# Odd heads' copies of k of three segments by DMA instead of by the vector engines, no unread products beside turns, and a new set of due times in an interleaved attention and feed-forward kernel

## The chip, the cores and the metric

The kernel runs on one core of a Trainium2 chip. The metric is device time in microseconds of one execution. Five engines work side by side, each through its own instruction stream in order: TensorE (PE, with its weight loads PEld), VectorE (DVE), ScalarE (ACT), GpSimd (POOL) and SyncE (SP), which here does nothing but issue DMAs.

## The reference, cut to what matters

Two blocks, A (attention with a memory, 32 heads of 16) and B (gated feed-forward), are applied twice in turn to x of 2048 x 512; inputs and outputs are bf16.

```
x = x + A(layernorm(x)); x = x + B(layernorm(x))     # and both once more

A: q, k, v = x @ wq, x @ wk, x @ wv                  # 32 heads, 16 columns each, 4 segments of 512 rows
   for s in 0..3:                                    # segments in order
       p = softmax(qs @ ks.T / 4 + causal mask)      # inside the segment
       a_dot = p @ vs
       a_mem = phi(qs) @ M / (phi(qs) @ z + 1e-6)    # what the earlier segments left
       o = g * a_mem + (1 - g) * a_dot               # g = sigmoid(beta), one per head
       M += phi(ks).T @ vs;  z += sum of phi(ks)
   return o @ wo
B: (gelu(x @ w_gate) * (x @ w_up)) @ w_down          # inner width 1792
```

## The kernel before, in words

One Python function, `order` (L286), writes out every engine's instruction stream itself. While it does so it keeps a clock for each engine (`Clocks`, L155) with fixed costs for each kind of instruction, and decides from these clocks what each engine gets next. The stream is fixed when the program is built; on the chip the engines follow it and wait for each other only through semaphores.

There are eight units of work, k = 0 to 7: four segments in the first application of A and B, four in the second (`Att` and `Ffn`). A segment has 512 rows in four tiles of 128. For each k:

- `Norm` makes statistics (`bn_stats`, `bn_aggr`), a scale on GpSimd, and normalized rows xn. These are turned into xnT either by a DMA transpose on SP's queue (`turn_later`) or, for the feed-forward of k = 0, 1 and 7, by TensorE (`turn_item`, L575). `turn_item` puts `FILL` = 2 products of the constant tile `warm` with nobody reading them ahead of each turn.
- q, k and v are projected (items of kind "qk" and "v") and evicted from PSUM by VectorE or ScalarE. Heads are kept in blocks of 128 rows, b = 0 to 3: each group of 32 rows holds an even head in rows 0 to 15 and an odd head in rows 16 to 31.
- `masked_copies` (L411) makes the tile kx from kf (the evicted k) by two multiplications with a mask of rows: one with the even heads' rows kept into columns 0 to C of each 3C (C = 64), one with the odd heads' rows kept into columns C to 3C. VectorE, GpSimd or ScalarE does both, whichever is free first. On VectorE and GpSimd the first copy writes 128 columns, of which the second overwrites the last 64. kx has two buffers (`kxs`) used by k in turn; for k = 0 it lies in the still empty tile of w_down. Event ("kB", k, b) says that it is there.
- `score_round` (L926) multiplies q with kf (even heads) or kx (odd heads, and both heads together) in 36 rounds of 256 columns, two rounds at a time: 18 pairs for each k. ScalarE takes the exponential (L1399), GpSimd masks the diagonal (L1346, L1351).
- `flush_item` (L943) multiplies the result with v (and with vz, a copy of halves of v that DMAs make) and hands it to VectorE for a transpose, a division and a transpose back. For k whose segment is not the first of four, the memory's part is added.
- The output projection ("wo"), the feed-forward's gate, up and down products follow. Gelu has its own phases on ScalarE.

What is ready is chosen by its due time, in units of k: `POLICY` (L69) holds some forty numbers, and `CHANGES` could give other numbers for each 20 us of the clocks, but is empty. A "qk" item is due at k - qk_due, a gate at k + gate_due + gate_step * ft, and so on; score rounds come before all others when their inputs, PSUM banks and buffers are free. Where no item is ready, the order puts in one unread product of `warm` (128 columns).

SP's queue carries, in this order of issue by its clock: loads of x and the weights, DMA transposes (xn, the exponentials of k, the memory's part), the copies for vz, and the stores. Pieces of w_o, w_gate and w_up are posted from 32 us, those of w_down after segment 0's scores.

```
PAIRED = [(ki, P * ki, C, C * ki) for ki in range(TPS)]
BY_PE = {("xnTf", 0), ("xnTf", 1), ("xnTf", NK - 1)}
FILL = 2
```

Of the kernel before, what the change touches and what calls it, by code (L numbers as in the profile page):

```python
# [18 lines left out]
P = 128  # L19
D = 512  # L20
# [11 lines left out]
VALUES = TPS * VW + 16  # L32
SCALE = DH ** -0.5
# [11 lines left out]
PAIRED = [(ki, P * ki, C, C * ki) for ki in range(TPS)]  # L45


def round_of(t):

    b, i = divmod(t, ROUNDS)  # L50
    if i == SHARED:
        return b, (0, 1), PAIRED, None
    par = int(i > SHARED)
    return b, (par,), FULL[i - par * (SHARED + 1)], DIAG[i - par * (SHARED + 1)]


BY_PE = {("xnTf", 0), ("xnTf", 1), ("xnTf", NK - 1)}
BANKS = 8
# [3 lines left out]
URGENT, SOON, NORMAL = -4.0, -1.5, 0.0  # L62
XN_BUFS = 4
BUFS = 6
FILL = 2
# [4 lines left out]
    flush_wait=60.178, piece_slack=2.474, kb_slack=40.846, mem_slack=-55.59, margin=2.052, qk_due=-2.997, e_q=-1.628,  # L70
    e_k=2.444, exp_slack=-52.211, e_slack=213.844, phi_slack=26.757, gelu_slack=17.711, act_evict=-7.207,
    first_evict=15.014, gate_step=70.271, up_due=-0.803, up_step=0.121, down_due=2.855, down_step=15.464,
    upd_due=-0.036, kb_act=30.625, vz_slack=-37.946, x_dve=-2.928, v0_due=-11.201, x1_at=-44.439, x2_at=17.127,
    x3_at=25.097, x3_load=11.502, direct=4, gelu_tiles=7, look=4.219, lag=0.576, wv_at=-5.253, xn_pool=39.635,
# [3 lines left out]
CHANGES = {  # L78
}
# [12 lines left out]
class Engine:  # L92
# [24 lines left out]
    def serve(self, now):  # L117
# [9 lines left out]
        job = min((j for j in jobs if j[0] + self.LATENCY <= start + 0.03), key=lambda j: j[0] + j[1] + (  # L127
# [123 lines left out]
class Item:  # L251


    def __init__(self, due, ready, ops, done, kind, ps, after="start"):
        self.after = after
        self.due = due if callable(due) else lambda: due
        self.ready, self.ops, self.done, self.kind, self.ps = ready, ops, done, kind, ps
        self.posted = 0.0
# [27 lines left out]
def order(pol, nc, cst, seg, wrk, psp, A_x, A_wq, A_wk, A_wv, A_wo, A_beta, B_x, B_w_gate, B_w_up, B_w_down, out):  # L286
# [88 lines left out]

    tmp_e2 = cst.tile([P, H], F32, name="tmp_e2")
# [26 lines left out]

    def on_dve_or_pool(ready, slack, later, fast, slow, emit, told):
# [6 lines left out]
    def masked_copies(ready, slack, kx, kf, told):  # L411
# [4 lines left out]
        def vector(which, eng):  # L416
            return lambda: eng.tensor_scalar(out=kx[:, :, C * which:C * which + P], in0=kf, scalar1=masks[:, which:which + 1],  # L417
                                             scalar2=None, op0=ALU.mult)
# [6 lines left out]
        ck.dve.post(ready, slack, (Port(0.35), vector(0, nc.vector), None),  # L425
                    (Port(0.35), vector(1, nc.vector), told), taken=taken)
        ck.pool.post(ready, slack + pol.kb_pool, (Port(1.57, True), vector(0, nc.gpsimd), None),
# [3 lines left out]
    def turn_later(t, slack, out, in_, landed, margin=0.0):  # L431
# [5 lines left out]
        ck.sp.post(t, slack, (1.3, lambda: nc.sync.dma_start_transpose(out=out(), in_=in_()), told))  # L437
# [40 lines left out]
    def soon(name, n=KT, part=1.0):  # L478

        t = ck.pe - 0.1 - ck.back  # L480
# [20 lines left out]
    class Norm:  # L501
        def __init__(self, key, tt0, tag, slack, free):
            self.key, self.tt0, self.tag, self.slack, self.free = key, tt0, tag, slack, free
            self.mv, self.n, self.left = None, 0, TPS
# [3 lines left out]

        def stats(self, j, ready):
            def emit():  # L510
                if self.mv is None:
                    self.mv = self.small("mv", 2)
# [3 lines left out]
            def told(t):  # L516
                self.n += 1
                if self.n == TPS:
                    self.scales(t)

            ck.dve.post(ready, self.slack, (0.66, emit, None),
# [1006 lines left out]
```

## Time and profile before

| | us |
|---|---|
| median of 3 runs (lowest to highest) | 542.2 (541.96 to 543.59) |
| the profiled execution, its own time | 543.32 |
| its span, first to last instruction | 541.6 |
| ScalarE's 288 exponentials (L1399), busy | 278.9 |
| VectorE's 18, GpSimd's 16 and ScalarE's 22 copies into kx, busy | 9.9, 27.0, 12.2 |
| SP's DMAs: 48 transposes of xn, median from issue to landing | 2.9 |

Times in the profile are counted from the span's start. A row of the timeline gives its start, its length, the engine and line, output and inputs, and in brackets how long the engine was idle before and what ended the idle time. A row of a window gives the stretch, its length, each engine's busy time in it with the number of instructions, the granted clock of TensorE (1.00 is full speed), the mean busy share of the DMA engines and GB/s. Matmuls are pipelined, and their busy time is modelled, so a busy TensorE is not one at its peak.

### The profile page before, as it was taken

What the parts mean: (1) busy time and instruction counts of PE and PEld (TensorE: products, weight loads), DVE (VectorE), ACT (ScalarE), POOL (GpSimd) and SP (SyncE); (2) the same over time, 40 slices, a digit from 0 to 9 for tenths busy, and PEclk for the clock granted to TensorE, in tenths of its full rate; (3) what the DMA queues carried; (4) which work ended last, traced back from release to release, by engine and by line L of the source; (5) the groups of instructions that cost most, each with busy time, mean ns of one, the idle gap of its engine ahead of it and who ended that gap; (6) DMA issues with size and microseconds to landing.
All of it is one profiled execution on the core that took longest, in us unless ns stands there. A gap on an engine that the chain in (4) does not pass through costs nothing.

```text
span 541.6 us, 22747 instructions
## 1 busy us (share of the span) xinstructions
PE 522.7 (97%) x10016; PEld 274.0 (51%) x10075; DVE 439.1 (81%) x814; ACT 434.3 (80%) x533; POOL 297.4 (55%) x346
## 2 busy tenths in 40 slices
PE   8899999999999999999999999999999999999997
PEld 4454555454554445554555545554465456555444
DVE  7899998899988998679987699879778786786342
ACT  5999899997998987999899899997887978910320
POOL 4887589487857986155871595716863164300000
PEclk9999999999999999999999999999999999999999
DMA  8477410620240124101332211411313014000001
GB/s 270 63 123 178 136 41 7 153 52 14 33 79 14 24 41 89 33 2 32 42 70 32 34 34 20 72 22 33 61 33 40 15 13 81 4 3 27 14 0 40
DMA packets 69141, 28.08 MB, mean 52 GB/s; under 512 B 53426, under 2 KB 69042, under 8 KB 69042
## 3 DMA queue, kind: packets, MB, share of 16 engines
q1 hardware_dynamic: 68752, 26.36, 24.5%
q8 instruction: 79, 1.29, 1.0%
q10 hardware_dynamic: 290, 0.26, 0.1%
q14 instruction: 20, 0.16, 0.1%
HBM read 9.70 MB, written 2.10 MB: 22 GB/s over the span
## 4 chain that ended last, share of the span: by engine, by line
PE 88%; DVE 6%; issue 2%; ACT 1%; DMA 1%; POOL 0%; ACTq 0%; DVEq 0%; POOLq 0%
PE ps L476 39%; PE ps L471 34%; PE ps L939 8%; PE ps L955 7%; ACT pt L1399 1%; DVE xn L544 1%; DMA xnT<-xn 1%; DVE st L514 1%; DVE x_sb L1028 1%; DMA x_sb<-in_A_x_dram 1%; PE ps L866 1%; DVE kx L417 0%; DVE st L1184 0%; DVE pt L1356 0%; DVE byq L972 0%
## 5 line engine op out<-in xcount | busy, mean ns | idle before, releaser
L1399 ACT ACTIVATE pt<-ps 128x1024 bf16<-128x1024 f32 x288 | 278.9, 1030 | 38.4 <-PE ps L939 34.1
L1346 POOL TENSOR_SCALAR_AFFINE_SELECT pt<-pt 128x256 bf16<-128x256 bf16 (+1 forms) x192 | 109.6, 584 | 132.5 <-ACT pt L1399 129.0
L1093 DVE TENSOR_TENSOR gel_sb<-gel_sb,ps 128x512 bf16<-128x512 bf16 x112 | 75.3, 683 | 33.8 <-PE ps L476 20.5
L1028 DVE TENSOR_TENSOR x_sb<-x_sb,ps 128x512 bf16<-128x512 bf16 (+1 forms) x68 | 43.1, 643 | 26.9 <-PE ps L476 16.4
L764 POOL TENSOR_SCALAR e<-e 128x512 bf16<-128x512 bf16 x39 | 61.4, 1577 | 4.6 <-ACT e L741 3.6
L476 PE MATMUL ps<-wd_sb,gel_sb 128*128 128x512 bf16 (+1 forms) x287 | 58.7, 351 | 1.5 <-issue 1.3
L972 DVE STREAM_TRANSPOSE byq<-ps 128x512 f32<-128x512 f32 x64 | 45.1, 706 | 16.1 <-PE ps L955 15.6
L471 PE MATMUL ps<-xnT,wg_sb 128*32 128x512 bf16 x916 | 56.1, 380 | 0.1
L476 PE MATMUL ps<-xnT,wu_sb 128*128 128x512 bf16 x213 | 51.1, 379 | 1.5 <-issue 1.1
L476 PE MATMUL ps<-xnT,wg_sb 128*128 128x512 bf16 x207 | 49.9, 379 | 1.6 <-issue 1.4
L471 PE MATMUL ps<-xnT,wu_sb 128*32 128x512 bf16 x888 | 51.0, 379 | 0.0
L471 PE MATMUL ps<-wd_sb,gel_sb 128*32 128x512 bf16 (+1 forms) x816 | 45.3, 361 | 0.0
L476 PEld LDWEIGHTS <-gel_sb 128*128 128x128 bf16 x300 | 27.9, 98 | 25.3 <-issue 0.4
L514 DVE BATCH_NORM_STATS2 st<-x_sb 128x6 f32<-128x512 bf16 x60 | 40.4, 673 | 0.2
L1351 POOL TENSOR_SCALAR_AFFINE_SELECT pt<-pt 64x1024 bf16<-64x1024 bf16 x26 | 32.4, 1247 | 9.8 <-ACT pt L1399 9.0
L955 PE MATMUL ps<-pt,vaug 128*32 128x256 bf16 (+2 forms) x1344 | 35.2, 238 | 1.5 <-issue 1.0
L471 PEld LDWEIGHTS <-wu_sb 128*32 128x32 bf16 x888 | 23.0, 97 | 22.3 <-issue 0.9
L955 PEld LDWEIGHTS <-vaug 128*32 128x32 bf16 x1344 | 27.6, 97 | 12.6 <-issue 4.1
L476 PEld LDWEIGHTS <-wu_sb 128*128 128x128 bf16 x226 | 20.8, 98 | 24.8 <-issue 1.2
L471 PEld LDWEIGHTS <-wg_sb 128*32 128x32 bf16 x916 | 23.4, 97 | 19.1 <-issue 1.3
L1152 ACT ACTIVATE gel_sb<-gel_sb 128x3584 bf16<-128x3584 bf16 (+1 forms) x14 | 32.4, 2351 | 0.0
L939 PE MATMUL ps<-q,kx 32*128 32x64 bf16 (+2 forms) x1120 | 31.2, 217 | 0.7 <-ACT pt L1399 0.5
(145 smaller groups left out, 892.7 us busy)
## 6 DMA issues: line engine op xcount, KB each, us to landing
vz<-vaug SPq DMA_DIRECT2D x14, 136.0 KB, 3.0
wg_sb<-in_B_w_gate_dram SPq DMA_DIRECT2D x8, 224.0 KB, 3.6
wu_sb<-in_B_w_up_dram SPq DMA_DIRECT2D x8, 224.0 KB, 2.9
wd_sb<-in_B_w_down_dram SPq DMA_DIRECT2D x7, 256.0 KB, 4.4
x_sb<-in_A_x_dram SPq DMA_DIRECT2D x3, 512.0 KB, 6.5
out_dram<-x_sb SPq DMA_DIRECT2D x12, 128.0 KB, 1.7
xnT<-xn SPq DMA_TRANSPOSE x48, 2.9
wk_sb<-in_A_wk_dram SPq DMA_DIRECT2D x2, 256.0 KB, 4.7
```

The costliest lines, as they stand in the source:

```text
L471: nc.tensor.matmul(out[r], lhsT=lhsT[:, r], rhs=rhs, start=start, stop=stop, tile_position=(0, 32 * c))
L476: nc.tensor.matmul(out, lhsT=lhsT, rhs=rhs, start=start, stop=stop)
L514: nc.vector.bn_stats(out=self.st6[:, 0, :], in_=x_sb[:, self.tt0 + j, :])
L764: lambda eng: eng.tensor_scalar(out=e[0][:], in0=e[0][:], scalar1=1.0, scalar2=None, op0=ALU.min), summed)
L939: nc.tensor.matmul(ps_all[:, bank, o + c0:o + c0 + n], lhsT=lhsT, rhs=self.q[rows, b, q0:q0 + n], start=True, stop=True, tile_position=(32 ...
L955: nc.tensor.matmul(ps()[32 * j:32 * j + 32, q0:q0 + n], lhsT=va[:, ki * VW + g:ki * VW + g + 32], rhs=pt_all[:, places[i], j, c0:c0 + n], ...
L972: nc.vector.transpose(out=self.byq[:, par, :, :].rearrange("p a c -> p (a c)"), in_=ps()[:])
L1028: ck.dve.post(ck.made(), slack, (0.15 + 0.00104 * (c1 - c0), lambda: nc.vector.tensor_tensor(out=xt, in0=xt, in1=ps()[:, 0:c1 - c0], op=AL ...
L1093: ck.dve.post(ck.made(), NORMAL, (0.683, lambda: nc.vector.tensor_tensor(out=g, in0=g, in1=ps()[:], op=ALU.mult), lambda t: (ps.read(t), e ...
L1152: return (0.205 + 0.427 * (f1 - f0), lambda: nc.scalar.activation(out=g, in_=g, func=ACT.Gelu_apprx_tanh), lambda t: self.gelu_done(t, f0, ...
L1346: nc.gpsimd.affine_select(out=view, in_=view, pattern=[[0, 4], [0, n], [1, C]], compare_op=ALU.is_ge, fill=0.0, base=C, channel_multiplier=-1)
L1399: nc.scalar.activation(out=pt_all[:, s0:s0 + 2, 2 * p:2 * p + 2, :].rearrange("p r h c -> p h r c"), in_=ps_all[:, pair[0]:pair[1] + 1, :] ...
```

## The change

1. For k = 1, 2 and 3 (`SENT`) the odd heads' rows of kx are no longer made by a masked multiplication. Four DMAs on SP's queue, one for each group of 16 rows, copy them from kf for all four blocks once all four are evicted. The rows of the even heads in these columns must be zero: VectorE zeroes them, for k = 1 and 3 (buffer 1) among the constants at the start, for k = 2 (buffer 0) in an instruction posted for 14 us. Later k in these buffers write the whole tile again by both masked copies.
2. The even heads' copy is 64 columns wide for each tile on every engine. For `SENT` it is the only one.
3. A round with odd heads waits for event ("kC", k, b) also, which the last of the four DMAs sets.
4. `FILL` is 0.
5. `POLICY` has other numbers, and `CHANGES` now has three further sets, from 80, 160 and 260 us.
6. Segment 0's gates from tile `HELD` = 5 on no longer wait for its memory update (tiles 0 to 4 of gel_sb hold segment 0's v until then), and its gates and ups are due in the order 5 to 13, 0 to 4. All gates wait until the first weights are there by the clock (`("loaded", "first")`), the down products for the last ones. An output projection waits for the half of aT that it reads.
7. Some costs of the clocks differ by a few hundredths (DMA issues 0.57 to 0.59 and 1.3 to 1.34).

Further code (tables of rounds by halves of a segment, statistics by ScalarE, a priority `CHAIN`) hangs on the tuple `HALVED`, which is empty, so that `table` gives the rounds and flushes of before.

```diff
-FILL = 2
+FILL = 0
+HELD = -(-VALUES // L)
+HALVED = ()
+SENT = (1, 2, 3)
...
-    flush_wait=60.178, piece_slack=2.474, kb_slack=40.846, mem_slack=-55.59, margin=2.052, qk_due=-2.997, e_q=-1.628,
+    flush_wait=1.624, piece_slack=0.155, kb_slack=53.547, mem_slack=-59.422, margin=2.0, qk_due=-7.042, e_q=-1.688,
...
-    kb_pool=0.131, cut_pool=-3.745, at_pool=5.073, pe_turns=0, gate_due=2.262, shun=0.829, col_gap=3.113, hold=3,
-    early=122.612, starve=0.322, near=-0.26, cap=2, soon=21.81, columns=0)
+    kb_pool=-10.364, cut_pool=0.647, at_pool=-5.829, pe_turns=0, gate_due=-18.64, shun=0.038, col_gap=0.385, hold=3,
+    early=105.4, starve=0.313, near=-1.083, cap=1, soon=20.189, columns=0, kd_slack=-0.023, zero_slack=2.11)
+STAGES = [
+    (4, 8, dict(
+        flush_wait=-28.356, piece_slack=0.165, kb_slack=13.812, mem_slack=-84.736, qk_due=-16.936, e_q=-16.571,
...
+        look=-0.727, lag=0.499, xn_pool=18.224, kb_pool=41.434, cut_pool=-4.43, at_pool=-1.122, gate_due=-0.69,
...
+    (8, 13, dict(
+        flush_wait=4.011, kb_slack=53.832, mem_slack=-53.484, qk_due=-18.021, e_q=-2.29, e_k=8.851, e_slack=302.471,
...
+        xn_pool=37.273, kb_pool=-1.463, cut_pool=-1.793, at_pool=-0.568, gate_due=-22.888, shun=-0.495, hold=0,
...
+    (13, 60, dict(
...
+        gate_due=2.674, shun=-0.495, hold=0, early=122.74, starve=0.322, near=-6.87, cap=0, soon=19.366,
+        kd_slack=2.0)),
+]
+CHANGES = {w: change for w0, w1, change in STAGES for w in range(w0, w1)}
...
+    nc.vector.memset(means[:, 0:1], -float(D) ** -1.5)
+    nc.vector.memset(means[:, 1:2], 1.0 / D)
+    nc.vector.memset(kxs[1][:, :, :, C:3 * C], 0.0)
...
+    ev["zero", 1] = ev["zero", 3] = 0.0
+    ck.dve.post(14.0, pol.zero_slack, (Port(0.95), lambda: nc.vector.memset(kxs[0][:, :, :, C:3 * C], 0.0),
+                                       lambda t: ev.update({("zero", 2): t})))
...
-    def masked_copies(ready, slack, kx, kf, told):
+    def masked_copies(ready, slack, kx, kf, even, told):
...
-            return lambda: eng.tensor_scalar(out=kx[:, :, C * which:C * which + P], in0=kf, scalar1=masks[:, which:which + 1],
-                                             scalar2=None, op0=ALU.mult)
+            n = P if which else C
+            return lambda: eng.tensor_scalar(out=kx[:, :, C * which:C * which + n], in0=kf[:, :, 0:n],
+                                             scalar1=masks[:, which:which + 1], scalar2=None, op0=ALU.mult)
...
+        if even:
+            ck.dve.post(ready, slack, (Port(0.28), vector(0, nc.vector), told), taken=taken)
+            ck.pool.post(ready, slack + pol.kb_pool, (Port(0.93, True), vector(0, nc.gpsimd), told), taken=taken)
+            ck.act.post(ready, slack + pol.kb_act, (0.51, scalar(0), told), taken=taken)
+            return
...
+            def sent():
+                parts = [32 * j + 16 for j in range(4)]
+                kf = self.kf[:].rearrange("p b (t c) -> p (b t) c", c=P)
+                kx = self.kx.rearrange("p b t c -> p (b t) c")
...
+                for r in list(parts):
+                    ck.sp.post(ck.pe, pol.kd_slack, (0.64, lambda r=r: nc.sync.dma_start(
+                        out=kx[r:r + 16, :, C:3 * C], in_=kf[r:r + 16, :, :]), told))
...
+                    if k in SENT:
+                        self.n_k += 1
+                        if self.n_k == KT:
+                            ck.at(t, lambda: ck.when(lambda: (k <= 2 or ("scores", k - 2) in ev) and ("zero", k) in ev, sent))
...
-                return Item(k + 0.61 + 0.001 * j, lambda: soon(("aT", k)),
-                            dense(ps, pairs), done, kind="wo", ps=ps, after=("aT", k, 3))
+                return Item(k + 0.61 + 0.001 * j, lambda: soon(("aTh", k, j // 2), eager=k in HALVED),
+                            dense(ps, pairs), done, kind="wo", ps=ps, after=("aTh", k, j // 2, 3))
...
-                return Item(lambda: -0.8 if phase[0] == k else k + pol.gate_due + pol.gate_step * ft,
-                            lambda: ck.has(("xnTf", k)) and (("down", k - 1) if k else ("upd", 0)) in ev,
+                return Item(lambda: -0.8 if phase[0] == k else k + pol.gate_due + pol.gate_step * place(ft),
+                            lambda: ck.has(("xnTf", k), ("loaded", "first")) and (k == 0 and ft >= HELD or (("down", k - 1) if k else ("upd", 0)) in ev),
```

More of the change, by code (lines that the diff above doesn't have):

```diff
@@ new lines, in second, with start @@
+                nc.gpsimd.tensor_tensor(out=self.rs[:, j0:j0 + n, :], in0=self.ve[:], in1=mhalf[:, 0:n, :], op=ALU.pow)
+            ck.pool.post(ready, min(self.urge(j0), URGENT), (0.25, first, None),
+                         (1.05, second, lambda t: ck.when(self.free, lambda: self.start(max(t, ck.pe), j0, n))))
+        def start(self, ready, j0, n):
+            if self.xnT is None:
+                self.xnT = seg.tile([P, KT, L], BF16, tag=self.tag, bufs=1, name="xnT")
+            for j in range(j0, j0 + n):
@@ L945, in flush_item @@
             ps = Psum()
-            number = 8 * k + 2 * b + par
+            places = self.places
+            half = L // 2
+            c0, c1 = (0, L) if h is None else (half * h, half * h + half)
+            na = (c1 - c0) // 32
+            work = []
+            for par in pars:
+                for t in used:
+                    for b2, par2, ki, q0, nq, o in TABLES[k][0][t][0]:
+                        if b2 == b and par in par2 and c0 <= q0 < c1:
+                            work.append((par, t, vz if len(par2) > 1 else self.vaug, ki, q0 - c0 + (par * half if h is not None else 0),
+                                         nq, o))
```

314 lines of the change are left out of this document (208 added, 106 removed).

## The prediction

> **What bounds the kernel now.** I read the page first: busy time and share of each engine, then the chain of waits.
>
> ```profile
> PE 522.7 (97%) x10016; PEld 274.0 (51%) x10075; DVE 439.1 (81%) x814; ACT 434.3 (80%) x533; POOL 297.4 (55%) x346
> ...
> PE 88%; DVE 6%; issue 2%; ACT 1%; DMA 1%; POOL 0%; ACTq 0%; DVEq 0%; POOLq 0%
> ```
>
> TensorE is 97% busy and 88% of the chain is its own work. An edit that frees VectorE, ScalarE or GpSimd is therefore worth only what TensorE lost by waiting for them. Where that was shows in the windows: busy us (with counts) of PE, PEld, DVE, ACT, POOL, then the clock, the DMA share and GB/s.
>
> ```profile
> 20.00:40.00 20.00, 18.28 (x427) 10.04 (x432) 18.61 (x44) 19.47 (x28) 16.84 (x19) 1.00 0.72 117
> 40.00:60.00 20.00, 19.57 (x360) 9.43 (x355) 19.27 (x35) 19.05 (x27) 13.10 (x15) 1.00 0.67 173
> 60.00:80.00 20.00, 18.61 (x462) 10.89 (x467) 19.06 (x40) 18.40 (x25) 15.42 (x18) 1.00 0.29 72
> 120.00:140.00 20.00, 18.35 (x481) 10.53 (x477) 19.57 (x40) 16.87 (x22) 16.18 (x21) 1.00 0.08 17
> 20.00:140.00 120.00, 114.01 (x2467) 61.66 (x2483) 111.84 (x215) 112.65 (x143) 91.23 (x99) 1.00 0.40 86
> 160.00:460.00 300.00, 293.56 (x6063) 152.92 (x6091) 250.58 (x455) 264.23 (x315) 173.47 (x201) 1.00 0.23 39
> ```
>
> Busy is not useful: with nothing ready the order emits products of the constant tile warm, which nobody reads. The windows of that tile alone (PE, PEld, DVE):
>
> ```profile
> 60.00:80.00 20.00, 2.59 (x54) 1.72 (x54) 0.00 (x0) 1.00 0.29 72
> 120.00:140.00 20.00, 1.88 (x29) 1.22 (x29) 0.00 (x0) 1.00 0.08 17
> 20.00:140.00 120.00, 6.93 (x126) 4.41 (x126) 0.00 (x0) 1.00 0.40 86
> 160.00:460.00 300.00, 0.00 (x0) 0.00 (x0) 0.00 (x0) 1.00 0.23 39
> ```
>
> I call idle plus unread products starvation. From 20 to 140 us it is 120 - 114.01 + 6.93 = 12.9 us; from 160 to 460 it is 300 - 293.56 = 6.4 us, or 0.43 per 20 us. At that plain rate 20 to 140 would cost 2.6, so **10.3 us** is all that a better supply can win. The two stretches that I price hold 20 - 18.61 + 2.59 - 0.43 = 3.55 us (60 to 80) and 20 - 18.35 + 1.88 - 0.43 = 3.1 us (120 to 140). The timeline says what they wait for:
>
> ```profile
> 64.73 1.46 PE L476 MATMUL ps<-wo_sb,aT 128*128 128x512 bf16 x6
> 66.12 0.40 PE L939 MATMUL ps<-q,kx 32*128 32x64 bf16 x20
> ...
> 71.79 0.51 PE L471 MATMUL ps<-warm 128*32 128x128 bf16 x24
> ...
> 78.80 1.55 PE L471 MATMUL ps<-xnT,wg_sb 128*32 128x512 bf16 x24
> ...
> 133.84 0.34 PE L471 MATMUL ps<-warm 128*32 128x128 bf16 x12
> ...
> 138.55 1.05 PE L471 MATMUL ps<-xnT,wg_sb 128*32 128x512 bf16 x16
> ```
>
> Unread products run from 71.8 until the first gate product of segment 0 at 78.8, and again from 133.8 to 138.5 before that of segment 1. The chain in front is: the segment's score rounds and their exponentials, P V, output projection (64.7), statistics, scale, normalized rows, turns, gate. It takes 14.1 us from the output projection to the gate alone.
>
> **The change part by part.** *Copies of k.* For segments 1 to 3, the windows of tile kx (PE, PEld, DVE, ACT, POOL) around their two places, then the whole window of the second place, ScalarE's two forms by themselves (busy us, mean ns), and VectorE's one (shortest, median, longest ns):
>
> ```profile
> 30.00:55.00 25.00, 0.00 (x0) 0.00 (x0) 4.39 (x8) 3.38 (x6) 3.24 (x2) 1.00 0.73 156
> 114.00:120.00 6.00, 0.00 (x0) 0.00 (x0) 1.31 (x2) 2.25 (x4) 3.13 (x2) 1.00 0.37 68
> ```
>
> ```profile
> 114.00:120.00 6.00, 5.95 (x146) 3.15 (x136) 5.39 (x11) 6.00 (x9) 5.90 (x7) 1.00 0.37 68
> ```
>
> ```profile
> L422 ACT ACTIVATE kx<-kf,masks 128x512 bf16<-128x512 bf16 x11 | 7.9, 719 | 0.0
> ...
> L422 ACT ACTIVATE kx<-kf,masks 128x256 bf16<-128x256 bf16 x11 | 5.6, 511 | 0.7 <-DVE kf L461 0.7
> ```
>
> ```profile
> L417 DVE TENSOR_SCALAR kx<-kf,masks x18: 332/566/820, 35.2 to 392.6; 128x512 bf16<-128x512 bf16 x18
> ```
>
> Twelve blocks lose the wide copy and keep one of 256 columns. On ScalarE, three blocks near 30 to 55 us: 3.38 - 3 x 0.511 = 1.85 us saved; two at 114 to 120: 2.25 - 2 x 0.511 = 1.23. VectorE shows no copy of 256 columns: it lies between half of 0.332 and 0.332; I take ScalarE's ratio, 0.511/0.719 x 0.332 = 0.24, since both shrink the same pattern. VectorE then saves 4.39 - 4 x 0.24 = 3.4 us in the first place. ScalarE is 97% and 95% busy around the first place (19.47 and 19.05 of 20), 100% at the second (6.00 of 6), and both lie ahead of a starved one, so I let ScalarE's 1.85 + 1.23 = **3.1 us** come off the two chains; each is less than the starvation behind it. Ends: 0, if VectorE's share of the chain is what sets it, and 4.6, with VectorE's 3.4 in the first place. The narrower first copies of the other segments save at most some 0.1 us each on VectorE; they lie where starvation is at the plain rate: nothing.
>
> *The zeroing.* Two memsets of 16 x 128 bf16 per partition. Nearest row: vz.
>
> ```profile
> 1.23 0.97 DVE L342 MEMSET vz<- 128x1096 uint32 x1 [0.18 <-issue]
> ...
> 2.48 0.15 DVE L374 TENSOR_REDUCE masks<-bd 128x1 f32<-128x4 f32 x1
> 3.72 0.69 DVE L1184 BATCH_NORM_STATS2 st<-x_sb 128x6 f32<-128x512 bf16 x1 [1.09 <-DMA x_sb<-in_A_x_dram]
> ```
>
> As 1024 words it takes 1024/1096 x 0.97 = 0.91 us; element by element, 2048/1096 x 0.97 = 1.82. The first stands in the hole of 1.09 us in which VectorE waits for x. With two memsets of a word or two in front, 0.91 just fits; 1.82 makes the first statistics, on which everything hangs, up to 0.8 late. I take 0.1. The second (posted for 14 us) is paid from the 3.4 just saved. The Trainium skill ("VectorE: DVE Perf Modes", "Zero memsets can be issued as uint32") says that such a zero over 2-byte elements can go as 4-byte words when its pattern reads as whole words, else a cycle per element. By the rule this pattern qualifies and the term is 0.1; by the plain element count it would be 0.8. The row agrees for a contiguous tile; none shows a strided one.
>
> *The twelve DMAs.* Each moves 16 partitions x 16 pieces x 256 B = 65.5 KB. Nearest rows:
>
> ```profile
> vz<-vaug SPq DMA_DIRECT2D x14, 136.0 KB, 3.0
> ```
>
> ```profile
> L701 SPq DMA_DIRECT2D vz<-vaug x14: 590/599/1262, 62.0 to 418.6; - x14
> ```
>
> ```profile
> 37.49 0.60 ACT L462 ACTIVATE kf<-ps 128x512 bf16<-128x512 f32 x1
> ```
>
> Four issues are 4 x 0.6 = 2.4 us of SP; landing 3.0 us later. Segment 1's last block of k is there at 37.49 + 0.60 = 38.1, so the odd heads land near 44, and the first round that reads them ran at 66.12: hidden by 22 us of other rounds. Were it late, that product would hold all of TensorE behind it. Where a group goes ahead of transposes of xn on SP, they come 2.4 us later; who waits are the next projections. Uncovered, three groups cost 7.2 us; TensorE starves hardly at all from 40 to 60 (0.43), so I take 0.
>
> *No unread products beside turns.*
>
> ```profile
> 494.84 0.21 PE L584 MATMUL ps<-warm 128*128 128x32 bf16 x2
> 494.90 0.38 PE L586 MATMUL ps<-ident,xn 128*128 128x128 bf16 x4
> ```
>
> ```profile
> 137.47 0.40 PE L586 MATMUL ps<-ident,xn 128*128 128x128 bf16 x4 [0.70 <-DVE xn L544]
> ```
>
> A pair costs 0.06 us where the row is ready (494.84 to 494.90), nothing where TensorE waits for it anyway (137.47). Twelve turns (four of three segments) have a pair each: 0 to 0.7; I take **0.4**.
>
> *The order.* New due times for the whole run, four sets by time; segment 0's gates from tile 5 on no longer wait for its memory update; an output projection may begin when its half is there. No row shows the new order. At most it wins the rest, 10.3 - 3.1 = 7.2; it can lose as much or more (rival 3). The gate rule alone gives nothing: the last turned rows come only just before 78.80. What can shrink is the 14.1 us to the gate: in it other products stand between the output projections (66.12). I take half of what is left in the two stretches, (3.55 + 3.1 - 3.1)/2 = **1.8 us**, because TensorE is in strict order and each step brought forward puts another back; with 0.4 from the smaller excess elsewhere, 2.2.
>
> *Sum.* -3.1 + 0.1 + 0 - 0.4 - 2.2 = -5.6 on the profiled execution of 543.32: 537.7. That execution lies 1.1 above the median 542.2, so **536.6**.
>
> **The rivals.** *1, the order removes all starvation above the plain rate.* 543.3 - 10.3 - 0.4 - 1.1 = 531.5. For: the losses stand in places that the order itself filled with unread products. Against: near 20 to 40 ScalarE is 97% busy, and no order mends that.
>
> *2, the hole is filled by something else.* ScalarE's freed time goes to other evictions, the chain is set by VectorE's statistics and normalized rows, and the new due times give back what they win: 542.2 - 0.4 = 541.8. For: VectorE is 95 to 98% busy from 60 to 80 and 120 to 140 as well.
>
> *3, dense work is spent too early (slower).* From 80 us on the projections' due time goes from k + 3 to k + 17 to 18, and from 160 to 260 us the first gate's from k + 2.3 to k - 22.9. If feed-forward products run as soon as they can, nothing is left to put beside the next segment's 18 pairs of rounds, and the boundaries of segments 2 to 6, which starve at the plain rate today, become like the first two: (3.55 + 3.1)/2 = 3.3 us each. It outweighs the gain from 5.6/3.3 = 1.7 boundaries on; with three of five, 536.6 + 9.9 = 546.5. For: 293.56 of 300 us leave little to win there and much to lose. Against: score rounds still come first, and the tail has dense work to spare.
>
> **How the numbers follow.** Forecast 0.47, rival 1 0.21, rival 2 0.12, rival 3 0.20. A measurement tells from no change what differs by over 0.3%, 1.6 us. Faster (under 540.6): 0.46 + 0.21 + 0.03 of rival 2 = 0.70. Same: 0.01 + 0.07 + 0.01 = 0.09. Slower (over 543.8): 0.02 of rival 2 and 0.19 of rival 3 = 0.21. The forecast's own range is 532.5 (order 4.5 instead of 2.2, copies 4.6, turns 0.7) to 540.4 (copies 0, memset 0.8). The whole goes down to 529, below rival 1 by the scatter of its plain rate, and up to 546, which takes in rival 2, rival 3 with up to two boundaries and part of the 7.2 us of late transposes.
>
> **What would show it.** Copies: kx on ACT at 256 columns only up to 140 us, and the first gate product before 77 instead of at 78.80. Memset: a row of 1024 words, with the first statistics still near 3.7. DMAs: four issues of 0.6 us, landed before 60. Order: starvation from 20 to 140 near 7 instead of 12.9. I am wrong if windows after 160 us hold unread products again or more than 0.43 idle (rival 3), or if the gates stay at 78.8 and 138.5 (rival 2).

## The result, and the profile after

The changed kernel took 540.91 us (median of 10 executions, 540.31 to 542.14), the kernel before 542.28 (10, 541.94 to 543.63): a ratio of 0.9972, 95% interval 0.9962 to 0.9982, or 1.4 us less. Forecast were 5.6 us less. Two later groups of 12 executions each gave 1.0004 and 0.9993, with intervals that hold 1 (experiments e9 and e13). By the three medians the change is therefore worth between 1.4 us and nothing; the widest interval, e9's, still allows a loss of 1.2 us.

The profiled execution took 540.6 us. Its page, busy time by engine and chain of waits:

```profile
span 538.4 us, 22807 instructions
...
PE 528.5 (98%) x10069; PEld 271.8 (50%) x10069; DVE 437.7 (81%) x817; ACT 430.6 (80%) x526; POOL 277.8 (52%) x342
...
PE 77%; ACT 1%; issue 0%; DVE 0%; ACTq 0%
```

The chain of after could be followed back only to 109.9 us, so its 77% for TensorE can't be set against the 88% of before. Form by form, copying and zeroing kx keeps GpSimd busy 23.6 us (27.0 before), ScalarE 10.2 (13.5) and VectorE 5.3 (9.9). In all GpSimd is busy 19.6 us less, ScalarE 3.7, VectorE 1.4; most of GpSimd's 19.6 is other work, of which the new order gives it less (its groups e<-e take 50.6 us instead of 61.4). The span is 3.2 us shorter (541.6 before), the profiled execution 2.7 us (543.32 before): 2.2 us now pass outside the span, where it was 1.7, and why isn't shown. The windows after (same columns as before):

```profile
20.00:40.00 20.00, 18.73 (x405) 9.78 (x404) 18.52 (x38) 19.80 (x27) 17.09 (x21) 1.00 0.45 86
40.00:60.00 20.00, 19.65 (x424) 9.96 (x423) 18.66 (x35) 19.23 (x25) 13.87 (x18) 1.00 0.68 179
60.00:80.00 20.00, 18.51 (x447) 9.91 (x446) 18.07 (x40) 17.39 (x25) 9.94 (x14) 1.00 0.54 107
...
120.00:140.00 20.00, 19.04 (x394) 10.67 (x390) 19.66 (x40) 17.04 (x22) 13.61 (x17) 1.00 0.11 24
...
160.00:460.00 300.00, 299.08 (x6428) 154.05 (x6421) 254.81 (x463) 264.58 (x314) 174.19 (x208) 1.00 0.21 39
20.00:140.00 120.00, 115.75 (x2386) 60.65 (x2385) 110.80 (x213) 111.29 (x139) 76.19 (x92) 1.00 0.41 92
```

And the windows of tile warm alone (PE, PEld, DVE):

```profile
60.00:80.00 20.00, 0.00 (x0) 0.00 (x0) 0.00 (x0) 1.00 0.54 107
...
120.00:140.00 20.00, 1.66 (x12) 0.76 (x12) 0.00 (x0) 1.00 0.11 24
20.00:140.00 120.00, 4.52 (x47) 2.39 (x47) 0.00 (x0) 1.00 0.41 92
```

Starvation (idle and unread) from 20 to 140 us is 120 - 115.75 + 4.52 = 8.8 us, not the 7 that were forecast. From 60 to 80 us no unread product is left, but TensorE idles for 1.49. The timeline of TensorE shows the two chains:

```profile
59.95 1.03 PE L558 MATMUL ps<-wo_sb,aT 128*128 128x512 bf16 x4
...
77.56 1.04 PE L553 MATMUL ps<-xnT,wg_sb 128*32 128x512 bf16 x16
...
123.53 1.03 PE L558 MATMUL ps<-wo_sb,aT 128*128 128x512 bf16 x4
...
138.63 2.55 PE L558 MATMUL ps<-xnT,wg_sb 128*128 128x512 bf16 x11
```

Segment 0's output projection starts 4.8 us earlier (64.73 before), its first gate product only 1.2 earlier (78.80 before): the way from the one to the other grew from 14.1 to 17.6 us. Segment 1's gate did not move (138.55 before).

The groups of tile kx (shortest, median and longest ns, first and last start in us) and then two rows of VectorE's timeline, the first zeroing and the first statistics:

```profile
L494 POOL TENSOR_SCALAR kx<-kf,masks x19: 915/995/1743, 39.3 to 388.6; 128x256 bf16<-128x256 bf16 x12, 128x512 bf16<-128x512 bf16 x7
L499 ACT ACTIVATE kx<-kf,masks x17: 505/549/758, 33.4 to 381.9; 128x256 bf16<-128x256 bf16 x10, 128x512 bf16<-128x512 bf16 x7
L798 SPq DMA_DIRECT2D kx<-kf x12: 586/622/712, 41.4 to 120.9; - x12
L494 DVE TENSOR_SCALAR kx<-kf,masks x8: 261/419/739, 34.7 to 325.6; 128x256 bf16<-128x256 bf16 x6, 128x512 bf16<-128x512 bf16 x2
```

```profile
2.81 0.91 DVE L447 MEMSET kx<- 128x1024 uint32 x1 [0.16 <-issue]
3.64 1.22 DVE L1367 BATCH_NORM_STATS2 st<-x_sb 128x6 f32<-128x512 bf16 x2
```

The prices were right but for one: the narrow copy costs 0.26 us on VectorE at its shortest (0.24 taken), an issue 0.62 (0.6), the zeroing 0.91 as 1024 words, and the first statistics start at 3.64. The DMAs into kx landed after a median of 3.9 us, where 3.0 had been taken.

### The profile page after: what moved, and what is told of

It is laid out like the page before. It is cut to its first block, busy times and chain, and to the rows that moved or that the text cites. A ratio compares the mean times of both kernels' runs of the same rounds, so it can differ in the third digit from the quotient of the medians.

```text
span 538.4 us, 22807 instructions
## 1 busy us (share of the span) xinstructions
PE 528.5 (98%) x10069; PEld 271.8 (50%) x10069; DVE 437.7 (81%) x817; ACT 430.6 (80%) x526; POOL 277.8 (52%) x342
## 4 chain that ended last, share of the span: by engine, by line
PE 77%; ACT 1%; issue 0%; DVE 0%; ACTq 0%
PE ps L558 33%; PE ps L553 31%; PE ps L1085 7%; PE ps L1114 6%; ACT pt L1588 1%; PE ps L1014 1%; ACT L1588 0%; PE ps L711 0%; ACT xnT L544 0%; DVE x_sb L1205 0%; ACTq L1588 0%
## 5 line engine op out<-in xcount | busy, mean ns | idle before, releaser
L558 PE MATMUL ps<-xnT,wg_sb 128*128 128x512 bf16 x303 | 71.3, 380 | 0.0
L912 POOL TENSOR_SCALAR e<-e 128x512 bf16<-128x512 bf16 x33 | 50.6, 1539 | 15.1 <-ACT e L889 14.4
L553 PE MATMUL ps<-xnT,wu_sb 128*32 128x512 bf16 x976 | 56.6, 379 | 0.0
L553 PE MATMUL ps<-wd_sb,gel_sb 128*32 128x512 bf16 (+1 forms) x1020 | 56.5, 361 | 0.0
L558 PE MATMUL ps<-wd_sb,gel_sb 128*128 128x512 bf16 (+1 forms) x249 | 50.2, 351 | 0.0
L558 PEld LDWEIGHTS <-wg_sb 128*128 128x128 bf16 x303 | 28.0, 98 | 31.6 <-issue 0.4
L553 PEld LDWEIGHTS <-gel_sb 128*32 128x32 bf16 x1020 | 25.8, 97 | 19.5 <-issue 2.0
L553 PE MATMUL ps<-xnT,wg_sb 128*32 128x512 bf16 x580 | 35.4, 380 | 0.0
L558 PEld LDWEIGHTS <-gel_sb 128*128 128x128 bf16 x249 | 23.2, 98 | 20.9 <-issue 0.9
L1335 ACT ACTIVATE gel_sb<-gel_sb 128x3584 bf16<-128x3584 bf16 (+3 forms) x15 | 32.6, 2211 | 0.0
```

Source lines behind the costliest of these rows:

```text
L553: nc.tensor.matmul(out[r], lhsT=lhsT[:, r], rhs=rhs, start=start, stop=stop, tile_position=(0, 32 * c))
L558: nc.tensor.matmul(out, lhsT=lhsT, rhs=rhs, start=start, stop=stop)
L912: lambda eng: eng.tensor_scalar(out=e[0][:], in0=e[0][:], scalar1=1.0, scalar2=None, op0=ALU.min), summed)
L1335: return (0.205 + 0.427 * (f1 - f0), lambda: nc.scalar.activation(out=g, in_=g, func=ACT.Gelu_apprx_tanh), lambda t: self.gelu_done(t, f0, ...
```

## The experiments

Each was timed beside the kernel before, and its ratio is to that. In e1 to e5 and e9 to e15 **the order is kept**: the clocks and costs from which `order` decides stay as they are, and only what it emits differs, so that every engine's other instructions keep their order (in e14 and e15 SP sends some DMAs later). In e6 to e8 the order is written anew.

| | order | copies of k | unread products | median us | ratio to before, interval |
|---|---|---|---|---|---|
| e1 | old | DMA, narrow | yes | 542.57 | 1.0000 (0.9986 to 1.0014) |
| e2 | old | masked, wide | no | 543.18 | 1.0006 (0.9992 to 1.0021) |
| e10 | old | DMA, narrow | no | 543.47 | 1.0012 (1.0003 to 1.0022) |
| e3 | new | masked, wide | no | 547.37 | 1.0077 (1.0061 to 1.0092) |
| e4 | new | masked, wide | yes | 547.14 | 1.0083 (1.0069 to 1.0098) |
| e11 | new | DMA, narrow | yes | 543.57 | 1.0018 (1.0004 to 1.0031) |
| after | new | DMA, narrow | no | 540.91 | 0.9972 (0.9962 to 0.9982) |
| e9, after again | new | DMA, narrow | no | 542.75 | 1.0004 (0.9986 to 1.0022) |
| e13, after again | new | DMA, narrow | no | 542.71 | 0.9993 (0.9977 to 1.0008) |
| e12 | new | DMA for GpSimd's blocks only | no | 544.52 | 1.0032 (1.0014 to 1.0049) |
| e5 | new, own tile | DMA, narrow | no | 543.02 | 1.0001 (0.9989 to 1.0013) |
| e14 | new, DMAs later | DMA, narrow | no | 541.38 | 0.9976 (0.9961 to 0.9991) |
| e15 | e14 and own tile | DMA, narrow | no | 541.63 | 0.9970 (0.9955 to 0.9986) |
| e6 | anew, old due times | DMA, narrow | no | 548.75 | 1.0122 (1.0095 to 1.0150) |
| e7 | anew, new due times | masked, first one narrow | no | 548.26 | 1.0105 (1.0088 to 1.0122) |
| e8 | anew, new due times | DMA, narrow | yes | 549.75 | 1.0127 (1.0112 to 1.0142) |

**The parts alone: e1 to e4.**

e1, on the kernel before:

```diff
+    nc.vector.memset(kxs[1][:, :, :, C:3 * C], 0.0)
+    ck.at(16.0, lambda: nc.vector.memset(kxs[0][:, :, :, C:3 * C], 0.0))
...
+            n = P if which else C
+            if sent and which:
+                return None
...
+                def odd_rows():
+                    self.n_copied += 1
+                    if self.n_copied == KT and k in (1, 2, 3):
...
+                        for r in [32 * j + 16 for j in range(4)][::-1]:
+                            nc.sync.dma_start(out=kx[r:r + 16, :, C:3 * C], in_=kf[r:r + 16, :, :])
```

> The instruction order of before, written out with its own costs; only the instructions differ: even heads' copies narrower, odd heads' rows of segments 1 to 3 by four DMAs each, two memsets. Theory A (the prediction's term: ScalarE's copies lie on the chains ahead of the first two gates): 3.1 us faster, 539.2. Theory B (the order fixes what stands beside what, so freed time on the other engines is not used by TensorE): within 0.8 us of 542.3. Theory C (the DMAs or the memset stand in the way): over 1 us slower.

e2, on the kernel before:

```diff
-            ops = [(Clocks.MM[512] / 2, whole(lambda: nc.tensor.matmul(
-                ps()[:, half:half + 32], lhsT=warm[:], rhs=wide[:, 0, 0:32], start=True, stop=True)))] * fill
+            ops = [(Clocks.MM[512] / 2, whole(lambda: None))] * fill
```

> The order of before without the 24 unread products beside turns. The prediction's term: 0.4 us faster, between 0 and 0.7. If they kept something fast behind them: slower.

e3, on the changed kernel:

```diff
-            ck.pool.post(ready, slack + pol.kb_pool, (Port(0.93, True), vector(0, nc.gpsimd), told), taken=taken)
+            ck.pool.post(ready, slack + pol.kb_pool, (Port(0.93, True), two(vector(0, nc.gpsimd), vector(1, nc.gpsimd)), told), taken=taken)
...
-                    ck.sp.post(ck.pe, pol.kd_slack, (0.64, lambda r=r: nc.sync.dma_start(
-                        out=kx[r:r + 16, :, C:3 * C], in_=kf[r:r + 16, :, :]), told))
+                    ck.sp.post(ck.pe, pol.kd_slack, (0.64, lambda: None, told))
```

> The order of the changed kernel, but both masked copies with the widths of before on the engine that the order names, no DMAs into kx, no memsets of kx. Theory A: 3.1 us slower than the changed kernel, 544.0. Theory B: about 541, as the changed kernel. If the new order was fitted to the short copies, more than 3 us slower.

e4, on e3: two products of `warm` ahead of each turn again.

> The order of the changed kernel with the instructions of before: masked copies and widths as in the run before this one, and two unread products ahead of each of the twelve turns. Difference to before is the order alone. Prediction: the order is worth -2.2 us, 540.1. Theory B: the order has nearly the whole gain, 541.3. Theory A with a losing order: above 543.

At the old order neither the copies nor leaving out the unread products shows a gain: e1 comes out as theory B said, and the intervals leave at most 0.8 us for e1 and 0.4 for e2. The new order alone costs 4.4 us (547.14 against 542.78 of its group); e3 and e4 come out as the last of their expectations. The short copies are thus worth nothing at the old order, and some 3.5 us at the new one (e4's ratio is 1.0083, e11's, with the same order and the short copies, 1.0018). What the freed time became in e1 is in its windows and in the list of what ScalarE waited for from 30 to 60 us (us in all, times, longest):

```profile
30.00:55.00 25.00, 25.00 (x490) 11.99 (x491) 22.41 (x39) 22.84 (x31) 17.05 (x19) 1.00 0.65 152
40.00:60.00 20.00, 19.82 (x363) 9.41 (x354) 18.53 (x32) 17.71 (x23) 11.07 (x14) 1.00 0.78 148
20.00:140.00 120.00, 116.00 (x2488) 61.45 (x2490) 109.40 (x205) 110.50 (x137) 87.10 (x97) 1.00 0.45 92
160.00:460.00 300.00, 298.51 (x6118) 153.54 (x6115) 250.04 (x455) 264.63 (x316) 170.04 (x202) 1.00 0.24 38
```

```profile
ACT pt L1415 <- PE ps L955: 2.0, 3, 1.0
```

ScalarE's busy time from 40 to 60 us fell from 19.05 to 17.71, and it now waits 2.0 us for TensorE's score rounds. TensorE runs them in a written order, and nothing in it was moved up. In the place of the first copies, 30 to 55 us, it is busy 25.00 of 25 us: there was no idle time to win. For the second place the prediction's own window said as much, 5.95 of 6.00. TensorE's gates, from e1's timeline, come 0.45 and 0.52 us earlier than before's:

```profile
78.35 2.56 PE L479 MATMUL ps<-xnT,wg_sb 128*32 128x512 bf16 x44
...
138.03 1.05 PE L479 MATMUL ps<-xnT,wg_sb 128*32 128x512 bf16 x16
```

The last of the windows corrects a reading of the prediction. e1 has the order of before, and TensorE is busy 298.51 of 300 us from 160 to 460; before's trace said 293.56. Before's page counts 10016 matmuls and 10075 weight loads, e1's 10075 of both: in before's trace matmul records are missing, and most of the "idle" 6.4 us was very likely that. By e1's trace (whose unread products from 20 to 140 take 6.93 us too) the old order starves for 120 - 116.00 + 6.93 = 10.9 us from 20 to 140. After's 8.8 is 2.1 less, and after's span is 540.7 - 538.4 = 2.3 us shorter than e1's. By stretches, from 60 to 80 us it is 2.2 less than in e1, from 120 to 140 0.8 less, and from 20 to 40 0.8 more.

One large part of what the new order loses without the short copies shows in e4's timelines of TensorE and of GpSimd, and in windows of 2 us:

```profile
50.46 0.40 PE L1119 MATMUL ps<-pt,gel_sb 128*32 128x64 bf16 x8 [2.15 <-POOL pt L1542]
```

```profile
41.54 4.79 POOL L493 TENSOR_SCALAR kx<-kf,masks 128x512 bf16<-128x512 bf16 x3
46.28 0.92 POOL L1542 TENSOR_SCALAR_AFFINE_SELECT pt<-pt 128x256 bf16<-128x256 bf16 x2
47.20 2.58 POOL L671 TENSOR_SCALAR xn<-x_sb,mv,rs 128x512 bf16<-128x512 bf16 x1
49.74 1.49 POOL L1542 TENSOR_SCALAR_AFFINE_SELECT pt<-pt 128x512 bf16<-128x512 bf16 x3
```

```profile
48.00:50.00 2.00, 0.30 (x16) 0.12 (x9) 0.60 (x1) 1.91 (x2) 2.00 (x2) 1.00 0.50 133
50.00:52.00 2.00, 1.54 (x36) 0.92 (x39) 0.84 (x2) 0.00 (x0) 2.00 (x4) 0.59 0.33 74
52.00:54.00 2.00, 2.00 (x29) 0.64 (x22) 1.97 (x4) 0.60 (x1) 1.91 (x2) 0.55 0.41 113
```

TensorE waits 2.15 us for GpSimd's mask of the diagonal, which starts at 49.74. Ahead of it GpSimd makes three wide copies without a break (4.79 us; two belong to a block, for which the order had counted one narrow copy of 0.93), two masks and a normalized row (2.58 us). After the wait TensorE's granted clock is at 0.59 and 0.55 for about 4 us. By an estimate from these windows the lower clock costs 2 x 0.41 + 2 x 0.45 = 1.7 us; with the wait that is 3.9 of the 7.7 us by which e4's span (546.1) is longer than after's. Where the rest goes isn't shown.

**Is it GpSimd: e12.** On the changed kernel, odd heads' DMAs only for blocks whose copy GpSimd makes; VectorE and ScalarE make both copies of theirs.

```diff
+            def both(f, g):
+                return lambda: (f(), g() if alone() else None)
...
-            ck.act.post(ready, slack + pol.kb_act, (0.51, scalar(0), told), taken=taken)
+            ck.act.post(ready, slack + pol.kb_act, (0.51, both(scalar(0), scalar(1)), told), taken=taken)
```

> The changed kernel with its order kept; of the twelve blocks only those whose copy GpSimd makes (5 of 12) get their odd heads by DMA, block by block; the others are made by VectorE and ScalarE with both masked copies, which the order does not count. With masked copies on all three engines this order took 547.4. Theory F (GpSimd's copies of 1.56 us each make the diagonal masks late, the product that waits for them leaves TensorE idle for 2 us near 48, and all that follows is late): with GpSimd relieved the wait near 50.5 is gone, and 541 to 543. Rival G (the surplus on ScalarE and VectorE carries the loss): 545 to 547.5.

544.52, between the two ranges. The wait of 2.15 us is gone and the clock stays at 1.00, as e12's windows of the same place show:

```profile
48.00:50.00 2.00, 1.84 (x53) 0.91 (x39) 1.92 (x5) 2.00 (x4) 1.42 (x3) 1.00 0.56 120
50.00:52.00 2.00, 2.00 (x10) 0.79 (x9) 2.00 (x4) 2.00 (x3) 0.66 (x2) 1.00 1.14 199
```

e12 is 0.32% above before where e3 was 0.77%: by these ratios GpSimd's copies carry some half of the loss. That the surplus on VectorE and ScalarE carries the rest is the reading that is left; e12 also sends other DMAs (16 smaller ones instead of 12), and no run separates the two. Seven of its eleven executions still had a mean granted clock under 0.999, so that the clock falls at other places too.

**The parts together: e10 and e11.** e10 is e1 and e2 in one; e11 puts the unread products back into the changed kernel.

> The kernel before with its order kept: copies of k by DMA and narrow, and no unread products beside turns, together. Each alone gave 0. Theory (TensorE's order sets the pace, and its strict order uses neither): 542.0 to 543.2, ratio 0.9985 to 1.0015. Rival (the unread products stood where the shorter copies would have let TensorE go on): 540.5 to 541.8.

> The changed kernel with its order kept and the 24 unread products ahead of the turns put back, the copies as changed. Theory (turns wait for their rows anyway): 0 to 0.4 above the changed kernel of this group. Rival (they cost their length, 24 x 0.03 and what stands behind them): 0.7 to 1.5 above it.

e10: no gain. Its ratio lies in the theory's range, its median 0.3 us above it, and its interval wholly above 1, which leaves a loss of 0.2 to 1.2 us. e11: 0.8 us above e9 of its group, as the rival said, but the intervals overlap, so that between the theory's 0.4 and the rival's 0.7 this doesn't decide.

Another rival is not settled: that the unread products keep TensorE's clock up. In e2, without them, six of twelve executions had a mean granted clock under 0.999, and four of the 23 of before beside it; but at the new order it was four of twelve with them (e11) and three of twelve without (e9).

**Writing the order anew: e6 to e8.**

e6 is the changed kernel with before's `POLICY` and this:

```diff
-CHANGES = {w: change for w0, w1, change in STAGES for w in range(w0, w1)}
+CHANGES = {}
```

> The changed kernel with the old single set of due times; the order is written anew with the odd heads' DMAs, the narrow copies and no unread products. Theory D (the order must know that the copies are short; the due times matter little once it does): the gain of 1.4 us is there, 540 to 541.5. Rival E (the due times were set for one exact set of costs, and the gain is theirs together with the copies): no gain or a loss, 541.8 to 546.

e7, on the changed kernel:

```diff
-SENT = (1, 2, 3)
+SENT = ()
```

> The changed kernel without the odd heads' DMAs: odd heads' copies are made by the engines again for all segments, with the cost that the order knows, so that it is written anew around them with the new due times. Theory D: the loss of 4.5 us that the new order showed with long copies it did not know of is mostly gone, since now it counts them; 541 to 543. Rival E: the due times do not carry over to another set of costs; 544 to 549.

e8, on the changed kernel:

```diff
-FILL = 0
+FILL = 2
```

> The changed kernel with two unread products ahead of each turn again, which the order counts and is written anew around. By the price of the products alone (0 at fixed order, at most 0.7 us): 540.5 to 541.8. Rival E: even so small an edit reshuffles the order, and the due times no longer fit: 544 to 549.

All three are 5.5 to 7 us slower than before; theory D fell in e6 and e7, the price of the products alone in e8. e6 and e8 lie above rival E's ranges too, by 2.75 and 0.75 us. The products that e8 adds cost 0.8 us by the medians where the order is kept (e11), and with the order written anew around them the kernel takes 549.75. That the due times fit one exact set of costs is the reading that is left; a single edit can't be priced here by rewriting the order around it.

**What ate the gain of segment 0: e5.** On the way from the output projection to the gate VectorE stood still for 1.43 us. After's row:

```profile
72.14 0.41 DVE L669 TENSOR_SCALAR xn<-x_sb,mv,rs 128x512 bf16<-128x512 bf16 x1 [1.43 <-DMA phik<-e]
```

The fourth normalized row waits for a buffer of a shared ring that a DMA transpose of the exponentials of k (phik<-e) still reads. e5 gives it a tile of its own:

```diff
-            xn = buffer(i, "xn")
+            xn = junk if self.key == ("xnTf", 0) and j == TPS - 1 else buffer(i, "xn")
```

> The changed kernel, its order kept; only the fourth normalized row of segment 0's feed-forward goes into a tile of its own instead of a buffer of the ring, so that it no longer waits for the transpose phik<-e that still reads the ring. Theory A (the 4.8 us won ahead of segment 0's output projection are lost again in the chain behind it, 1.4 of them to this wait): the wait of 1.43 us at 72.14 is gone, the first gate product comes at 76.1 to 76.6 instead of 77.56, and the median falls by 0.9 to 1.4 from 540.9 to 539.5 to 540.0. Rival C (another wait ends there too: the PSUM bank or VectorE's other rows): the gate stays within 0.4 of 77.56 and the median within 0.4 of 540.9.

The wait is gone and the gate comes at 77.22 instead of 77.56, which is rival C: TensorE's turns end at 73.14 instead of 74.21, and then it waits in one piece for the next thing, an exponential of ScalarE. Its row in e5:

```profile
74.54 0.66 PE L1014 MATMUL ps<-gel_sb,phik 128*32 128x32 bf16 x64 [1.41 <-ACT pt L1588]
```

In after there were two waits, 0.79 for the turns and 0.68 here. They add up to about the same. The median, 543.02, lies above both ranges and 0.3 us above e9's 542.75; e5's group had no unaltered changed kernel.

The 4.8 us were not all lost. From the output projection to the gate TensorE is busy 16.1 of 17.6 us in after, with no unread product; before it was busy 12.8 of 14.1, and 2.5 of that were unread products. So it starves there for 1.5 us instead of 3.8: other segments' products stand in the longer way.

**The same kernel again, and its DMAs later: e9, e13 to e15.** e9 and e13 are the changed kernel unaltered, both on one chip. e14, with SP's order alone changed:

```diff
-                    ck.sp.post(ck.pe, pol.kd_slack, (0.64, lambda r=r: nc.sync.dma_start(
-                        out=kx[r:r + 16, :, C:3 * C], in_=kf[r:r + 16, :, :]), told))
+                    def send(r=r):
+                        nc.sync.dma_start(out=kx[r:r + 16, :, C:3 * C], in_=kf[r:r + 16, :, :])
+
+                    ck.sp.post(ck.pe, pol.kd_slack, (0.64, lambda send=send: ck.at(ck.pe + (20.0, 8.0)[k - 2], send) if k > 1 else send(), told))
```

e15 is e14 with e5's tile.

> The changed kernel as it is, once more, beside the three others of this group on the same chip. If its gain is a property of the kernel, the ratio to the kernel before is 0.996 to 0.9985 again, 540 to 541.5; if it belonged to the chip or the day, 0.9985 to 1.0015. It is also what the run with the fourth row's own tile is to be held against: that row's wait was gone and the gate came 0.34 us earlier, and the median should be 0 to 0.4 below this one.

> The changed kernel as it is, as the measure for the two others of this group. Theory H (its gain of 1.4 us at first and of nothing the second time differ by DMAs that land earlier or later): between 540.5 and 543, with TensorE waiting up to 1.2 us for phik<-e near 119 where the median landing of the transposes there is over 3.5 us, and not waiting where it is under 3.

> The changed kernel with the order of the other four engines kept; SP issues the DMAs into kx of segment 2 some 20 us later and those of segment 3 some 8 us later (they are read from 115 and 175 us on), behind the transposes and the copies into vz. Theory H (these DMAs delay the transposes phik<-e and w_up's pieces): no wait for phik<-e near 119, and a median 0.4 to 1.2 us below the changed kernel of this group. Rival (the transposes land late by themselves): within 0.4 us of it.

> As the kernel before it in this group, and the fourth normalized row of segment 0's feed-forward in a tile of its own. By the gate of 0.34 us earlier that this tile gave: 0.2 to 0.5 us below that kernel. If the two waits hide each other: the same as that kernel.

e9's 1.0004 is what was expected if the first gain belonged to the chip or the day; e9 and e13 can't tell these from chance. e14 is 1.3 us below e13, just over theory H's range, and e15 1.1; both lie under before with their whole interval, which e9 and e13 do not. Their intervals overlap e13's. e15 is no faster than e14, so e5's tile adds nothing here. SP's queue in after, in its order of issue:

```profile
58.74 1.27 SPq L798 DMA_DIRECT2D kx<-kf  x2
60.11 1.37 SPq L849 DMA_DIRECT2D vz<-vaug  x2
61.53 1.31 SPq L798 DMA_DIRECT2D kx<-kf  x2
62.88 2.67 SPq L372 DMA_DIRECT2D wu_sb<-in_B_w_up_dram  x4
65.66 6.63 SPq L519 DMA_TRANSPOSE phik<-e  x3
```

The same stretch in e14, and its normalized rows on VectorE:

```profile
60.42 2.64 SPq L372 DMA_DIRECT2D wu_sb<-in_B_w_up_dram  x4
63.16 9.27 SPq L519 DMA_TRANSPOSE phik<-e  x3
72.47 3.02 SPq L799 DMA_DIRECT2D kx<-kf  x4
```

```profile
69.19 1.84 DVE L669 TENSOR_SCALAR xn<-x_sb,mv,rs 128x512 bf16<-128x512 bf16 x4
```

With segment 2's copies out of the way SP reaches the transposes 2.5 us sooner, and the wait of 1.43 us before the fourth row is gone: four rows in one go. In e13 that wait was longer. Its row on VectorE, and TensorE's windows behind it:

```profile
72.76 0.41 DVE L669 TENSOR_SCALAR xn<-x_sb,mv,rs 128x512 bf16<-128x512 bf16 x1 [1.80 <-DMA phik<-e]
```

```profile
72.00:74.00 2.00, 0.88 (x32) 0.69 (x32) 1.24 (x3) 0.51 (x2) 0.33 (x1) 1.00 0.59 67
74.00:76.00 2.00, 1.42 (x80) 1.22 (x81) 1.93 (x5) 2.00 (x3) 1.48 (x1) 1.00 0.00 0
76.00:78.00 2.00, 2.00 (x30) 0.62 (x19) 2.00 (x6) 1.57 (x4) 0.69 (x2) 0.52 0.04 8
78.00:80.00 2.00, 2.00 (x36) 0.94 (x36) 0.93 (x3) 1.61 (x3) 0.00 (x0) 0.62 0.00 0
```

TensorE idles for 1.7 us in 4, then its clock is at 0.52 and 0.62 for the next 4, and the gate comes at 79.66, later than before's.

How much of the 1.3 us is the wait itself? Five of e13's twelve executions had a mean clock of 0.997, none of e14's twelve was under 0.999. Among the executions at 0.999 and more the medians are 541.72 (e13, seven) and 541.38 (e14), 0.3 us apart; and e14's gate comes at 77.23, 0.33 us before after's, just as in e5. So the wait itself is worth some 0.3 us, and the rest comes with the lower clock. That sending these DMAs later is what keeps the clock up isn't shown: e5, on another chip, lacks the wait as well, and eight of its twelve executions had the lower clock.

At the second place, near 119 us, theory H does not hold. In e9 TensorE waits for the transpose there, in e13 too (0.94 us), and in e15, whose copies of segment 3 are sent after it, likewise; a row of e9 and one of e15:

```profile
120.31 0.56 PE L1014 MATMUL ps<-vaug,phik 128*32 128x32 bf16 x52 [1.08 <-DMA phik<-e]
```

```profile
120.09 0.56 PE L1016 MATMUL ps<-vaug,phik 128*32 128x32 bf16 x52 [0.93 <-DMA phik<-e]
```

The transposes issued from 106 to 125 us landed after a median of 2.8 us in after and e14, 3.7 in e9, 4.1 in e13 and 4.3 in e15, and TensorE waits where it was over 3.5, as expected of e13. These copies are not what decides the landing; why it differs between executions of one order stays open.

## Why the prediction was right and wrong

**Right:** the direction of the first measurement and the range (529 to 546 holds all three groups, but it is wide enough to hold nearly any outcome); the prices of single instructions, but for the landing of the DMAs; the place of the starvation; that the gates of later segments lose nothing (299.08 of 300 busy from 160 to 460 us, so no rival 3). All three medians lie where the prediction's own measure says "same" (540.6 to 543.8), and it gave that 0.09.

**The step that failed first** is "I let ScalarE's 1.85 + 1.23 = 3.1 us come off the two chains". ScalarE's time did become free, and e1 shows that it turned into ScalarE's waiting for TensorE. An engine that is 97% busy ahead of a starved stretch was taken for the one that sets it; but at a fixed order TensorE sets the pace of the score rounds (busy 25.00 of 25 us in e1 while the copies are made), and the measured term is 0 (at most 0.8 by e1's interval), the end that the prediction had named for another reason.

**The order's 2.2** was added to that as if the two were separate. They are not: 0 for the copies, +4.4 for the order alone, -1.4 to 0 for both. The short copies are the condition under which the new order doesn't lose. Copies and order together were to take 3.1 + 1.8 = 4.9 us of starvation out of the two stretches, and 0.4 elsewhere; set against e1's trace, starvation fell by 2.9 us in the two stretches and rose by 0.8 from 20 to 40 us. Segment 1's gate stayed where it was (138.63).

**The DMAs' 0** was not right. The prediction had the mechanism ("they come 2.4 us later"; e14 shows 2.5) but looked only at starvation from 40 to 60 us and at who waits for xn; the late ones are the transposes phik<-e, and behind them a buffer for the fourth normalized row, on the starved chain. e14 puts it at some 0.3 us by itself and 1.3 with the lower clock that e13 had and e14 had not, inside the bound of 7.2; neither is clear of the scatter.

**The turns' 0.4** can't be told from 0 (e2) or 0.8 (e11). **The memset's 0.1** was at most that. The "plain rate" of 0.43 per 20 us was very likely mostly missing records. The bound of 10.3 that was made with it holds by luck: e1's trace gives 10.9, less 0.6 at its own plain rate (1.49 us of 300), which is 10.3 again.

**The rivals.** Measured were 540.9 to 542.75, nearest to rival 2 with its 541.8. Its mark, gates that stay, shows for segment 1 only, and its mechanism only in part: ScalarE's freed time was not passed to other evictions in e1 but spent waiting, and segment 0's hole was filled by other segments' products, which is a gain and not a loss.

## What to carry to other kernels

Here, time freed on an engine that feeds TensorE was worth nothing until TensorE's own order was moved up to use it, so price such an edit together with the order it needs, and test it at the order of before as well as at its own. A DMA that is "hidden" because its reader comes late still stands in a queue ahead of others: look for who waits behind it, and send it where the queue is empty. The start of one product is a poor measure of a chain: compare how much useful work stands before it. A gain of a quarter of a per cent is worth measuring on a second occasion before it is explained.

## What the runs showed of the hardware that was not expected

Short waits of TensorE can cost a second time. One wait of 2.15 us in e4 and 1.7 us of idle within 4 in e13 were each followed by about 4 us at a granted clock of 0.52 to 0.62; in e10 four waits adding up to 1.6 us (133.6 to 136.9 us) come with windows at 0.70 and 0.50 (136 to 140 us). By an estimate from e13's two windows that is 2 x 0.48 + 2 x 0.38 = 1.7 us, 0.3% of the span, so a mean clock of 0.997 stands for one such stretch; e13's executions with 0.997 were 1.8 us longer in the median than its others. The Trainium skill (TensorE: Matmul & The Clock Gate, section "Why this matters for your kernels") warns of idle gaps above some 3 us; here the lower clock followed shorter ones, but not always: e5's profiled execution kept a clock of 1.00 behind its 1.41 us. Of the 24 executions of e9 and e13 eight had a mean clock under 0.999, eight of e5's twelve, and none of the 24 of e14 and e15, which idle nearly as long at that place (e14: 1.47 us); what decides is open.

The DMA transposes that follow one another on one queue landed in 2.4 to 4.5 us in the same stretch of the same work (106 to 125 us, in after, e9 and e13 to e15). Whether this, the clock or the chip makes the changed kernel's three medians differ isn't shown.
